# Joining the two words of a float64 weight with integer operations: six passes for ten

## The chip, the cores and the metric

The kernel runs on one core of a Trainium2 chip as one program. The time is the device time of that core in microseconds (us), the median over the runs. Five engines work at the same time, each through its own instructions in a fixed order: TensorE (PE, with its weight loads shown apart as PEld), VectorE (DVE), ScalarE (ACT), GpSimd (POOL) and SyncE (SP). SP does nothing here but issue DMAs. An instruction waits for what it needs on semaphores, and what stands behind it on the same engine waits too.

## The reference, cut to what matters

Three stages follow each other. The attention stage first lets 32 packed queries attend to 576 keys for each of 4 x 8 heads, and then lets the 576 queries attend to the 32 results. Its output, 2304 tokens of 512 values, goes through a first MoE layer and then through a second one with eight experts and an iterated routing:

```
p_packed = sm_attn(p, k, v); out = sm_attn(q, p_packed, p_packed)
h = x @ w_in                              # 512 -> 2048
x = (h * clip(h + 3, 0, 6) / 6) @ w_out   # 2048 -> 512
P = routing of x @ w_gate
out = sum over 8 experts of P[:, e] * (relu(x @ w1[e]) @ w2[e])
```

The two weight matrices of the first layer, `w_in` (512 x 2048) and `w_out` (2048 x 512), come as float64: 8 bytes for each element, 16.8 MB together. All else is float32.

## The kernel before, in words

**The planner.** The program is not written in the order in which it runs. Each operation is put into `Order` with an assumed cost on an engine (`t_act`, `t_dve`, `t_pool`, `t_pe`), with the buffers it reads, writes and fills, and with a priority (a smaller number goes first). `Order.run` then takes, again and again, the operation that can start first by those assumed costs, and among equals the one with the smaller priority. That gives every engine its order of instructions, SP's queue of loads included. An operation made with `alt` may go to POOL or to DVE; it goes to DVE if it would end there earlier by a margin. A buffer is a slot of a small set (`place`); a new use of a slot waits until the last user of the old one has ended. So a change in what an operation is assumed to cost, or in which buffers it holds, moves the order of other work on all engines.

**Start of the program.** Eight attention units (two for each of four batches) load their `k`, `q` and `v` (L510, L527, L535), transpose them on PE through PSUM tiles `tp` (L557, L647, L667), and work through two softmaxes on DVE and ACT. A small copy `pd` on POOL (L543) and a masked copy `pt` on DVE (L579) stand ahead of each unit's first scores (L599). Meanwhile the weights of the groups 0 to 3 of the first layer are loaded and converted ("early" pieces). The first layer has 8 groups of 256 of the 2048 inner values, and a unit of its work (`layer1a`, `layer2a`: L890 to L892 and L928 to L930 on PE) takes 384 tokens and two groups. PE multiplies with each operand split into a high and a low part, three products for one. The attention stage has a higher priority than the matmuls of the first layer, which fill what PE has left over. The groups 4 to 7 are converted while the first layer runs. After it comes the second layer (L996 to L998 and L1055 to L1057), with float32 weights.

**The conversion.** A raw piece `raw` of 128 partitions x 512 values of 8 bytes (512 KB) is one DMA on SP's queue (L392). There are two slots for `raw`, so the third load waits until the first piece has been used for the last time, and what stands behind it in SP's queue, the loads of `k`, `q` and `v` too, waits with it. There are 32 pieces: 16 early ones, each converted as one split of 512 values in `m_early` tiles, and 16 later ones, each as two splits of 256 values in `m` tiles. So there are 16 splits of 512 and 32 splits of 256. Each split holds two tiles (`m` and `t`) out of four.

The high word of a float64 holds the sign, 11 bits of exponent and the top 20 bits of the fraction; the low word holds 32 more bits. A split takes ten passes before. ACT makes the absolute value of the high word, read as if it were a float32 (L353), its sign (L357), and the low word as a number times 2 to the -52 (L361). DVE clamps the absolute value to the range of float32 exponents (L364), shifts it left by three and flips two bits (L367), ACT clears the sign bit (L371), and DVE masks the power of two out (L373). Three joins (L348, on POOL or DVE) multiply the low part by that power, add it, and multiply by the sign. For `w_in` the result lies in `w1f`; for `w_out` it is then split into a high part (L428, ACT) and a low part (L433, POOL or DVE). A `raw` slot comes free after the last join of its piece.

Of the kernel before, what the change touches and what calls it, by code (L numbers as in the profile page):

```python
# [9 lines left out]
F32 = mybir.dt.float32  # L10
F32R = mybir.dt.float32r
AF = mybir.ActivationFunctionType
ALU = mybir.AluOpType
# [3 lines left out]
U32 = mybir.dt.uint32  # L17


def float_of(bits):  # L20
    return struct.unpack("f", struct.pack("I", bits))[0]


def as_f32(ap):
    return ap.bitcast(F32)
# [32 lines left out]
JOIN = 0.5  # L58
# [75 lines left out]
def t_dve(n, fast=False):  # L134
    return 0.065 + n / (1920.0 if fast else 960.0)


def t_act(n, psum=False):
    return (0.05 if psum else 0.095) + n / 1200.0


def t_pool(n):
    return 0.15 + n / 465.0
# [7 lines left out]
def tile_kernel(  # L151
# [16 lines left out]
    nc = tc.nc  # L168
# [20 lines left out]
    def pool(name, stack=ctx, **kw):  # L189
        return stack.enter_context(tc.tile_pool(name=name, bufs=1, **kw))  # L190

    const, dp, accp, hp, wp = (pool(n) for n in ("const", "dp", "accp", "hp", "wp"))
    ph = pool("ph", space=PSUM)
    one, two = ctx.enter_context(ExitStack()), ctx.enter_context(ExitStack())
# [68 lines left out]
    maskb = const.tile([128, 2, NP], F32, name="maskb")  # L263
    maskz = const.tile([128, 2, 2, D], F32, name="maskz")
    three = const.tile([128, 1], F32, name="three")

    order = Order()

# [9 lines left out]
    def hold(tag, shape, dt=F32):  # L278
        return Hold(res[tag], maker(tag, shape, dt, ("",)))
# [8 lines left out]
    def dve(cost, fn, **kw):  # L288
        return order.op([("DVE", cost, fn)], **kw)

    def act(cost, fn, **kw):
        return order.op([("ACT", cost, fn)], **kw)

    def gps(cost, fn, **kw):
        return order.op([("POOL", cost, fn)], **kw)
# [14 lines left out]
    def alt(cost_dve, cost_pool, fn, spare=0.0, **kw):  # L310

        return order.op(
            [
                ("POOL", cost_pool, lambda: fn(nc.gpsimd)),
                ("DVE", cost_dve, lambda: fn(nc.vector), spare),
            ],
            **kw,
        )
# [7 lines left out]
    LEAST = float_of(897 << 20)  # L326
    MOST = float_of(0x47EFF000)
# [7 lines left out]
    def split_f64(r, c0, n, w, at, prio, halves, tag):  # L335

        words = lambda i: r.t.bitcast(U32).rearrange("p (n t) -> p n t", t=2)[:, c0:c0 + n, i]
        m = hold(tag, [128, n], U32)  # L340
        t = hold(tag, [128, n], U32)
        fast = t_dve(n, True)
        kw = dict(prio=prio)
        ts = nc.vector.tensor_scalar

        def join(dst, i0, i1, how, **deps):
            return alt(
                t_dve(n), t_pool(n), lambda e: e.tensor_tensor(dst(), i0(), i1(), how),  # L348
                spare=JOIN, **deps, **kw,
            )  # L350

        first = act(
            t_act(n), lambda: nc.scalar.activation(as_f32(m.t), as_f32(words(1)), AF.Abs),  # L353
            reads=[r], writes=[m], takes=[t], **kw,
        )
        sign = act(
            t_act(n), lambda: nc.scalar.activation(as_f32(words(1)), as_f32(words(1)), AF.Sign),  # L357
            takes=[r], after=[*r.writers[:1], first], **kw,
        )
        rest = act(  # L360
            t_act(n), lambda: nc.scalar.activation(as_f32(words(0)), words(0), AF.Copy, scale=2.0 ** -52),  # L361
            takes=[r], after=r.writers[:1], **kw,
        )
        dve(fast, lambda: ts(as_f32(m.t), as_f32(m.t), LEAST, MOST, ALU.max, ALU.min), writes=[m], **kw)  # L364
        dve(
            fast,
            lambda: ts(t.t, m.t, 3, 0xC0000000, ALU.logical_shift_left, ALU.bitwise_xor),  # L367
            reads=[m], writes=[t], **kw,
        )
        act(  # L370
            t_act(n), lambda: nc.scalar.activation(as_f32(t.t), as_f32(t.t), AF.Abs), writes=[t], **kw  # L371
        )
        dve(fast, lambda: ts(m.t, t.t, 0xFF800000, None, ALU.bitwise_and), reads=[t], writes=[m], **kw)  # L373
        mf, tf = (lambda: as_f32(m.t)), (lambda: as_f32(t.t))
        join(mf, lambda: as_f32(words(0)), mf, ALU.mult, takes=[r], writes=[m], after=[rest])
        join(tf, tf, mf, ALU.add, reads=[m], writes=[t])
        if halves:
            join(tf, tf, lambda: as_f32(words(1)), ALU.mult, takes=[r], writes=[t], after=[sign])
            split_part(at, tf, w, n, [t], prio)
        else:  # L380
            join(
                lambda: at(w.t), tf, lambda: as_f32(words(1)), ALU.mult,
                takes=[r], reads=[t], fills=[w], after=[sign],
            )

    def raw_piece(src, prio, tag="raw"):

# [9 lines left out]
    def whole(g, which, prio, tag, early=False):  # L397

        _, w1, w2, f0 = groups[g]
        if which == "w1":  # L400
            src = w1[:, f0:f0 + FG].rearrange("(c p) f -> p c f", p=128)
        else:
            src = w2[f0:f0 + FG, :].rearrange("(c p) d -> p c d", p=128)
        wide = src.dtype == I64
        shape = list(src.shape)
        w = hold(tag, shape) if which == "w1" else pair(tag, shape)
        per = shape[1] // (2 if wide else 1)
        for i in range(0, shape[1], per):
            r = raw_piece(src[:, i:i + per, :], prio, turn_of("raw", early))

            def at(t, i=i, c0=0, n=per * shape[2]):
                return t[:, i:i + per, :].rearrange("p c n -> p (c n)")[:, c0:c0 + n]

            if wide:
                n = DEC_EARLY if early else DEC
                for c0 in range(0, per * shape[2], n):
                    split_f64(
                        r, c0, n, w, lambda t, at=at, c0=c0, n=n: at(t, c0=c0, n=n), prio, which == "w2",
                        "m_early" if early else "m",
                    )  # L420
            else:
                split_part(at, lambda r=r: r.t, w, per * shape[2], [r], prio)
        return w

    def split_part(dst, src, w, n, deps, prio, **kw):

        high = act(
            t_act(n), lambda: nc.scalar.activation(dst(w.t[0]), src(), AF.Copy),  # L428
            reads=deps, fills=[w], prio=prio, **kw,
        )  # L430
        return alt(
            t_dve(n), t_pool(n),
            lambda e: e.tensor_tensor(dst(w.t[1]), src(), as_f32(dst(w.t[0])), ALU.subtract),  # L433
            reads=deps, fills=[w], after=[high], prio=prio, spare=SPARE,
        )
# [776 lines left out]
    with tc.manual_schedule():  # L1212
        nc.vector.memset(ones, 1.0)
        nc.vector.memset(three, 3.0)
        nc.vector.memset(maskb, 0.0)
        nc.vector.memset(maskb[0:64, 0, :], 1.0)
        nc.vector.memset(maskb[64:128, 1, :], 1.0)
# [20 lines left out]
        for gg in range(4):  # L1238
# [7 lines left out]
            writes=[wg], prio=90,  # L1246
# [81 lines left out]
```

## Time and profile before

| what | value |
|---|---|
| median of 3 runs | 1955.41 us (1952.35 to 1956.96) |
| span of the profiled execution | 1952.2 us |
| PE busy | 1915.1 us, 98% of the span |
| DVE, ACT, POOL busy | 62%, 50%, 49% |
| granted TensorE clock, mean | 0.998 |

The span reaches from the first to the last instruction of the profiled execution. The profile gives no separate device time for that execution; its span is 0.15 us under the fastest of the three runs and 3.2 us under their median. Busy shares are means over stages that differ: the conversion that is changed runs only in the first 310 us.

### The profile page before, as it was taken

How to read it: one execution, taken by the hardware profiler on the slowest of the kernel's cores; microseconds unless marked ns; L12 is line 12 of the kernel's file. 1: busy time of each engine (PE TensorE's matmuls, PEld its weight loads, DVE VectorE, ACT ScalarE, POOL GpSimd, SP SyncE). 2: the span in 40 equal slices, each digit the busy share in tenths (PEclk: the TensorE clock that was granted, in tenths of full speed). 3: DMA queues.
4: the chain of work that ended last, by engine and by line, in shares of the span. 5: the costliest groups of instructions: out<-in, count | busy, mean ns of one | idle time of the engine just before them, and what ended most of it. 6: DMA issues, size and time to landing. Idle time of an engine off the chain costs nothing.

```text
span 1952.2 us, 28194 instructions
## 1 busy us (share of the span) xinstructions
PE 1915.1 (98%) x10573; PEld 1735.2 (89%) x10573; DVE 1210.0 (62%) x1998; ACT 970.2 (50%) x2135; POOL 947.5 (49%) x987
## 2 busy tenths in 40 slices
PE   6999999999999999999999999999999999999998
PEld 4789999998899999999899999999999999999997
DVE  6996686447866676666755555555555555555554
ACT  6885674335455555555544443344444344443432
POOL 2444675236665666655634544435344343444431
PEclk9999999999999999999999999999999999999999
DMA  9931121001222222222310101111110111101102
GB/s 215 188 90 33 54 66 44 11 1 44 65 65 66 75 65 70 71 65 65 87 33 33 44 22 44 33 33 33 33 44 30 36 33 33 44 22 44 33 11 66
DMA packets 103546, 104.87 MB, mean 54 GB/s; under 512 B 42736, under 2 KB 78576, under 8 KB 103408
## 3 DMA queue, kind: packets, MB, share of 16 engines
q1 hardware_dynamic: 103408, 103.06, 19.4%
q8 instruction: 83, 1.36, 0.3%
q14 instruction: 55, 0.45, 0.1%
HBM read 98.32 MB, written 4.72 MB: 53 GB/s over the span
## 4 chain that ended last, share of the span: by engine, by line
PE 91%; DVE 5%; ACT 2%; DMA 1%; issue 1%; SPq 0%; POOL 0%; DVEq 0%; POOLq 0%; ACTq 0%
PE po L1055 13%; PE po L1056 13%; PE po L1057 13%; PE ph L996 12%; PE ph L998 12%; PE ph L997 12%; PE po L928 3%; PE po L930 3%; PE po L929 3%; PE ph L890 2%; PE ph L892 1%; PE ph L891 1%; PE ph L841 1%; DMA raw<-in_moe_w_out_dram 1%; DVE tmp L908 0%
## 5 line engine op out<-in xcount | busy, mean ns | idle before, releaser
L1079 DVE SCALAR_TENSOR_TENSOR acc<-po,Pr,acc 128x512 f32<-128x512 f32 x504 | 377.3, 750 | 287.2 <-PE po L1057 284.1
L433 POOL TENSOR_TENSOR hsl<-tmp,hsh 128x384 fp32r<-128x384 f32 x382 | 391.8, 1031 | 325.4 <-ACT hsh L428 272.4
L1055 PE MATMUL po<-w2h,hsh 128*128 128x512 f32 x1152 | 449.0, 390 | 0.0
L1056 PE MATMUL po<-w2l,hsh 128*128 128x512 f32 x1152 | 448.8, 390 | 0.0
L1057 PE MATMUL po<-w2h,hsl 128*128 128x512 f32 x1152 | 448.6, 389 | 0.0
L433 POOL TENSOR_TENSOR w1xl<-m,w1xh 128x256 fp32r<-128x256 f32 x152 | 111.5, 758 | 321.8 <-ACT w1xh L428 321.8
L1057 PEld LDWEIGHTS po<-w2h,hsl 128*128 128x128 f32 x1152 | 216.2, 188 | 45.3
L304 ACT ACTIVATE tmp<-ph 128x384 f32<-128x384 f32 x241 | 117.7, 489 | 274.8 <-PE ph L998 263.1
L1055 PEld LDWEIGHTS po<-w2h,hsh 128*128 128x128 f32 x1152 | 216.3, 188 | 41.8 <-DVE acc L1079 0.2
L1056 PEld LDWEIGHTS po<-w2l,hsh 128*128 128x128 f32 x1152 | 216.3, 188 | 41.5
L428 ACT ACTIVATE hsh<-tmp 128x384 fp32r<-128x384 f32 x480 | 242.4, 520 | 20.4 <-DVE tmp L908 12.6
L1010 DVE TENSOR_TENSOR tmp<-ph,tmp 128x384 f32<-128x384 f32 x288 | 159.8, 556 | 149.3 <-PE ph L998 129.7
L428 ACT ACTIVATE w2h<-raw 128x1024 fp32r<-128x1024 f32 x64 | 67.9, 1061 | 350.1 <-PE po L1057 338.1
L1018 ACT ACTIVATE tmp<-tmp 128x384 f32<-128x384 f32 x288 | 149.6, 520 | 87.2 <-DVE tmp L1010 82.8
L996 PE MATMUL ph<-ax,w1h 128*128 128x384 f32 x448 | 151.5, 338 | 3.3 <-DVE tmp L1010 3.3
L998 PE MATMUL ph<-ax,w1l 128*128 128x384 f32 x448 | 150.7, 336 | 0.0
L997 PE MATMUL ph<-ax,w1h 128*128 128x384 f32 x448 | 150.7, 336 | 0.0
L433 DVE TENSOR_TENSOR hsl<-tmp,hsh 128x384 fp32r<-128x384 f32 x98 | 105.6, 1078 | 42.0 <-ACT hsh L428 39.8
L433 POOL TENSOR_TENSOR w1l<-raw,w1h 128x512 fp32r<-128x512 f32 (+1 forms) x104 | 116.3, 1132 | 7.5 <-ACT w1h L428 6.8
L996 PE MATMUL ph<-xyh,w1h 128*128 128x384 f32 x320 | 108.3, 339 | 3.6 <-ACT tmp L304 3.6
L455 POOL TENSOR_TENSOR m<-raw 128x256 f32<-128x256 f32 x58 | 44.5, 770 | 138.7 <-DMA raw<-in_moe_w_dram 136.0
L998 PE MATMUL ph<-xyh,w1l 128*128 128x384 f32 x320 | 108.1, 338 | 0.0
(207 smaller groups left out, 4040.4 us busy)
## 6 DMA issues: line engine op xcount, KB each, us to landing
raw<-in_moe_w_dram SPq DMA_DIRECT2D x128, 512.0 KB, 3.5
raw<-in_moe_w_in_dram SPq DMA_DIRECT2D x16, 512.0 KB, 3.9
raw<-in_moe_w_out_dram SPq DMA_DIRECT2D x16, 512.0 KB, 3.6
k<-in_k_dram SPq DMA_DIRECT2D x32, 144.0 KB, 5.9
q<-in_q_dram SPq DMA_DIRECT2D x32, 144.0 KB, 4.5
v<-in_v_dram SPq DMA_DIRECT2D x8, 576.0 KB, 6.5
out_dram<-acc SPq DMA_DIRECT2D x36, 128.0 KB, 2.3
p<-in_p_dram SPq DMA_DIRECT2D x1, 224.0 KB, 5.7
```

What stands on the lines that cost most here:

```text
L304: ("ACT", t_act(n, True), lambda: nc.scalar.activation(dst(), src(), AF.Copy)),
L428: t_act(n), lambda: nc.scalar.activation(dst(w.t[0]), src(), AF.Copy),
L433: lambda e: e.tensor_tensor(dst(w.t[1]), src(), as_f32(dst(w.t[0])), ALU.subtract),
L996: nc.tensor.matmul(out, wh[:, at + c, :], bh[:, c, :], start=first and c == 0, **on)
L997: nc.tensor.matmul(out, wh[:, at + c, :], bl[:, c, :], start=False, **on)
L998: nc.tensor.matmul(out, wl[:, at + c, :], bh[:, c, :], start=False, **on)
L1010: t_dve(n), lambda: nc.vector.tensor_tensor(u.t, ps.t[:, :n], u.t, ALU.add),
L1018: t_act(n, bool(ps)), lambda: nc.scalar.activation(c.t, src(), AF.Relu),
L1055: nc.tensor.matmul(ps.t, hh[:, f, ts], wh[:, f, :], start=(f == 0), stop=False)
L1056: nc.tensor.matmul(ps.t, hh[:, f, ts], wl[:, f, :], start=False, stop=False)
L1057: nc.tensor.matmul(ps.t, hl[:, f, ts], wh[:, f, :], start=False, stop=(f == NFC - 1))
L1079: lambda row=row, share=share, ps=ps: nc.vector.scalar_tensor_tensor(row(), ps.t, share(), row(), ALU.mult, ALU.add),
```

## The change

The sum of a shifted high word and a rounded low word now makes the float directly, as an integer. ACT turns the low word into `2.0 + low * 2^-51` (a float whose bit pattern is 0x40000000 plus the low word's top bits, rounded), with the 2.0 as a bias out of a new tile `two`, and makes the absolute value of the high word as before. DVE clamps as before and shifts left by three, now without the flip. A new DVE operation with three operands takes the sign bit of the high word and sets it into the rounded low word. An integer add on POOL joins the two. This add has no choice of engine. `raw` is last read by the new DVE operation.

```diff
-        def join(dst, i0, i1, how, **deps):
-            return alt(
-                t_dve(n), t_pool(n), lambda e: e.tensor_tensor(dst(), i0(), i1(), how),
-                spare=JOIN, **deps, **kw,
-            )
-        first = act(
+        def join(dst, **deps):
+            return gps(
+                t_pool(n), lambda: nc.gpsimd.tensor_tensor(dst(), m.t, t.t, ALU.add), **deps, **kw,
+            )
+        low = act(
+            t_act(n) + 0.1,
+            lambda: nc.scalar.activation(as_f32(words(0)), words(0), AF.Identity, bias=two_, scale=2.0 ** -51),
+            takes=[r], after=r.writers[:1], **kw,
+        )
+        act(
             t_act(n), lambda: nc.scalar.activation(as_f32(m.t), as_f32(words(1)), AF.Abs),
             reads=[r], writes=[m], takes=[t], **kw,
         )
-        sign = act(
-            t_act(n), lambda: nc.scalar.activation(as_f32(words(1)), as_f32(words(1)), AF.Sign),
-            takes=[r], after=[*r.writers[:1], first], **kw,
-        )
-        rest = act(
-            t_act(n), lambda: nc.scalar.activation(as_f32(words(0)), words(0), AF.Copy, scale=2.0 ** -52),
-            takes=[r], after=r.writers[:1], **kw,
-        )
         dve(fast, lambda: ts(as_f32(m.t), as_f32(m.t), LEAST, MOST, ALU.max, ALU.min), writes=[m], **kw)
+        dve(fast, lambda: ts(m.t, m.t, 3, None, ALU.logical_shift_left), writes=[m], **kw)
         dve(
-            fast,
-            lambda: ts(t.t, m.t, 3, 0xC0000000, ALU.logical_shift_left, ALU.bitwise_xor),
-            reads=[m], writes=[t], **kw,
-        )
-        act(
-            t_act(n), lambda: nc.scalar.activation(as_f32(t.t), as_f32(t.t), AF.Abs), writes=[t], **kw
-        )
-        dve(fast, lambda: ts(m.t, t.t, 0xFF800000, None, ALU.bitwise_and), reads=[t], writes=[m], **kw)
-        mf, tf = (lambda: as_f32(m.t)), (lambda: as_f32(t.t))
-        join(mf, lambda: as_f32(words(0)), mf, ALU.mult, takes=[r], writes=[m], after=[rest])
-        join(tf, tf, mf, ALU.add, reads=[m], writes=[t])
+            t_dve(n),
+            lambda: nc.vector.scalar_tensor_tensor(
+                t.t, words(1), 0x80000000, words(0), ALU.bitwise_and, ALU.bitwise_or
+            ),
+            takes=[r], writes=[t], after=[low], **kw,
+        )
         if halves:
-            join(tf, tf, lambda: as_f32(words(1)), ALU.mult, takes=[r], writes=[t], after=[sign])
-            split_part(at, tf, w, n, [t], prio)
+            join(lambda: t.t, reads=[m], writes=[t])
+            split_part(at, lambda: as_f32(t.t), w, n, [t], prio)
         else:
-            join(
-                lambda: at(w.t), tf, lambda: as_f32(words(1)), ALU.mult,
-                takes=[r], reads=[t], fills=[w], after=[sign],
-            )
+            join(lambda: at(w.t).bitcast(U32), reads=[m, t], fills=[w])
...
+        nc.vector.memset(two_, 2.0)
```

## Rows read from the trace of the kernel before

**Rows 1.** Page: busy us, share of the span and instructions of each engine.

```profile
PE 1915.1 (98%) x10573; PEld 1735.2 (89%) x10573; DVE 1210.0 (62%) x1998; ACT 970.2 (50%) x2135; POOL 947.5 (49%) x987
```

**Rows 2.** Windows: PE, PEld, DVE, ACT, POOL busy, clock, DMA share, GB/s.

```profile
0.00:14.00 14.00, 2.86 (x13) 2.06 (x14) 8.25 (x22) 7.34 (x13) 2.42 (x8) 1.00 0.98 205
14.00:40.00 26.00, 20.74 (x220) 14.92 (x221) 18.26 (x52) 17.31 (x47) 7.62 (x10) 1.00 1.08 220
40.00:80.00 40.00, 35.19 (x375) 27.47 (x376) 36.37 (x98) 35.13 (x93) 20.71 (x19) 1.00 1.00 194
110.00:150.00 40.00, 38.11 (x287) 34.02 (x282) 36.57 (x78) 32.82 (x76) 19.49 (x20) 1.00 0.27 81
250.00:310.00 60.00, 58.54 (x360) 54.03 (x359) 55.02 (x106) 42.92 (x109) 45.24 (x53) 1.00 0.23 68
310.00:1952.20 1642.20, 1629.82 (x8390) 1481.55 (x8388) 963.90 (x1460) 748.76 (x1592) 783.47 (x804) 1.00 0.15 44
```

**Rows 3.** Waits of PE, first 150 us: total us, times, longest.

```profile
PE tp L557 <- DMA k<-in_k_dram: 9.9, 3, 7.8
PE tp L599 <- DVE pt L579: 2.1, 2, 1.8
PE tp L574 <- POOL pd L543: 1.4, 2, 0.9
```

**Rows 4.** Waits of SP's queue, first 150 us.

```profile
SPq L392 <- DVE m_early L348: 14.5, 4, 9.5
SPq L392 <- DVE w1f L348: 12.8, 4, 8.9
```

**Rows 5.** Timeline: start, us, engine, line, operation [idle before <-releaser].

```profile
12.96 0.69 DVE L348 TENSOR_TENSOR w1f<-m_early,raw 128x512 f32<-128x512 f32 x1
13.57 0.28 DVE L579 TENSOR_TENSOR pt<-tp,maskb 128x128 f32<-128x128 f32 x1
...
27.86 0.35 SPq L392 DMA_DIRECT2D raw<-in_moe_w_out_dram  x1
...
35.60 0.27 PE L557 MATMUL tp<-ident,k 96*128 96x96 f32 x1 [1.56 <-DMA k<-in_k_dram]
```

**Rows 6.** Windows of L348 alone: DVE and POOL busy in each.

```profile
0.00:140.00 140.00, 22.58 (x26) 27.61 (x21) 1.00 0.79 167
140.00:310.00 170.00, 26.84 (x32) 50.59 (x66) 1.00 0.19 56
```

**Rows 7.** Groups by line and form: times, busy us, mean ns; the other removed passes.

```profile
L357 ACT ACTIVATE raw<-raw 128x512 f32<-128x512 f32 x16 | 11.0, 689 | 0.0
L371 ACT ACTIVATE m_early<-m_early 128x512 f32<-128x512 f32 x16 | 10.2, 639 | 0.3 <-DVE m_early L367 0.2
L373 DVE TENSOR_SCALAR m_early<-m_early 128x512 uint32<-128x512 uint32 x16 | 8.8, 552 | 1.5 <-ACT m_early L371 1.1
L357 ACT ACTIVATE raw<-raw 128x256 f32<-128x256 f32 x32 | 14.1, 440 | 0.5
L371 ACT ACTIVATE m<-m 128x256 f32<-128x256 f32 x32 | 13.3, 416 | 14.0 <-DVE m L367 13.6
L373 DVE TENSOR_SCALAR m<-m 128x256 uint32<-128x256 uint32 x32 | 13.4, 417 | 5.7 <-ACT m L371 5.3
```

**Rows 8.** Instructions of the tiles: ns min/median/max, first and last start.

```profile
L348 DVE TENSOR_TENSOR m_early<-raw,m_early x10: 682/693/1674, 8.4 to 137.7; 128x512 f32<-128x512 f32 x10
L348 POOL TENSOR_TENSOR m_early<-raw,m_early x6: 1295/1306/1312, 30.3 to 123.3; 128x512 f32<-128x512 f32 x6
L348 DVE TENSOR_TENSOR m<-raw,m x9: 414/923/1287, 186.7 to 291.7; 128x256 f32<-128x256 f32 x9
```

**Rows 9.** Groups by form: an activation with a bias tile, and one without.

```profile
L903 ACT ACTIVATE tmp<-ph,three 128x384 f32<-128x384 f32 x96 | 55.5, 578 | 87.3 <-PE ph L892 86.2 <-DVE ax L433 0.8
L937 ACT ACTIVATE acc<-po 128x384 f32<-128x384 f32 x24 | 11.6, 484 | 6.1 <-PE po L930 6.0
```

**Rows 10.** DMA issues, first 140 us: KB each, median us to landing.

```profile
raw<-in_moe_w_out_dram SPq DMA_DIRECT2D x8, 512.0 KB, 4.8
```

More of the change, by code (lines that the diff above doesn't have):

```diff
@@ L265, in tile_kernel @@
     three = const.tile([128, 1], F32, name="three")
+    two_ = const.tile([128, 1], F32, name="two")
     order = Order()
@@ L355, in split_f64 @@
         )
-        sign = act(
-            t_act(n), lambda: nc.scalar.activation(as_f32(words(1)), as_f32(words(1)), AF.Sign),
-            takes=[r], after=[*r.writers[:1], first], **kw,
-        )
-        rest = act(
-            t_act(n), lambda: nc.scalar.activation(as_f32(words(0)), words(0), AF.Copy, scale=2.0 ** -52),
-            takes=[r], after=r.writers[:1], **kw,
-        )
-        dve(fast, lambda: ts(as_f32(m.t), as_f32(m.t), LEAST, MOST, ALU.max, ALU.min), writes=[m], **kw)
-        dve(
-            fast,
-            lambda: ts(t.t, m.t, 3, 0xC0000000, ALU.logical_shift_left, ALU.bitwise_xor),
-            reads=[m], writes=[t], **kw,
-        )
-        act(
-            t_act(n), lambda: nc.scalar.activation(as_f32(t.t), as_f32(t.t), AF.Abs), writes=[t], **kw
-        )
-        dve(fast, lambda: ts(m.t, t.t, 0xFF800000, None, ALU.bitwise_and), reads=[t], writes=[m], **kw)
-        mf, tf = (lambda: as_f32(m.t)), (lambda: as_f32(t.t))
-        join(mf, lambda: as_f32(words(0)), mf, ALU.mult, takes=[r], writes=[m], after=[rest])
-        join(tf, tf, mf, ALU.add, reads=[m], writes=[t])
+        dve(fast, lambda: ts(as_f32(m.t), as_f32(m.t), LEAST, MOST, ALU.max, ALU.min), writes=[m], **kw)
+        dve(fast, lambda: ts(m.t, m.t, 3, None, ALU.logical_shift_left), writes=[m], **kw)
+        dve(
+            t_dve(n),
[3 more added lines that the diff above has]
+            takes=[r], writes=[t], after=[low], **kw,
+        )
         if halves:
-            join(tf, tf, lambda: as_f32(words(1)), ALU.mult, takes=[r], writes=[t], after=[sign])
-            split_part(at, tf, w, n, [t], prio)
-        else:
-            join(
-                lambda: at(w.t), tf, lambda: as_f32(words(1)), ALU.mult,
-                takes=[r], reads=[t], fills=[w], after=[sign],
-            )
+            join(lambda: t.t, reads=[m], writes=[t])
+            split_part(at, lambda: as_f32(t.t), w, n, [t], prio)
+        else:
+            join(lambda: at(w.t).bitcast(U32), reads=[m, t], fills=[w])
     def raw_piece(src, prio, tag="raw"):
```

## The prediction

> **What bounds the kernel now.** I read the page first, then the windows by stage, then who waits for whom on PE and on SP's queue, and last the single passes of the conversion.
>
> PE is busy for 1915.1 of 1952.2 us [rows 1], so all its idle time is 37.1 us, and a change to the conversion can gain no more than the part of it that the conversion causes. The windows say where it lies [rows 2]: 11.1 us in the first 14 us, 5.3 from 14 to 40, 4.8 from 40 to 80, 1.9 from 110 to 150, 1.5 from 250 to 310, and 12.4 after 310, where nothing is converted any more. The granted clock is 1.00 in all these stretches but the last, so there is nothing to win from the clock.
>
> Of the first 14 us, 9.9 us in three waits (one of them later) are PE waiting for the first `k` loads [rows 3]; the change does not touch their start. The other 1.8 us there is one wait for `pt` on DVE [rows 3]. `pt` stands behind joins of the conversion in DVE's order: one ends as `pt` begins [rows 5], and two more of the same kind run in front of that one. So the idle time in reach is 1.8 + 5.3 + 4.8 + 1.9 + 1.5 = 15.3 us, 0.8% of the whole. That is the ceiling, however much work the change removes.
>
> Which engine makes PE wait in those stretches? From 40 to 80 us DVE is busy 36.4 of 40 us and ACT 35.1; from 110 to 150 DVE 36.6 of 40; from 250 to 310 DVE 55.0 of 60 [rows 2]. There DVE is close to full, and attention's small steps, which PE needs, stand in its order between conversions. From 14 to 40 DVE has 18.3 of 26 us and ACT 17.3: no engine is full; the DMA share is 1.08, and PE waits for loads and for chains of small steps. In that stretch the conversion acts through SP's queue: SP waits for the last join before it may load the next `raw`, 14.5 us and 12.8 us in eight waits for joins on DVE alone [rows 4], and loads of `k` and `q` stand behind. One case can be followed to PE: SP loads `raw` at 27.86 as soon as a join has ended, the next `k` goes after it, and PE waits 1.56 us for `k` at 35.60 [rows 5].
>
> **The change part by part.** Early splits (16 of 512 values, to about 140 us):
> - ACT loses the sign and the second absolute value, 11.0 + 10.2 = 21.2 us [rows 7]. The low word's pass stays, but gets a bias tile. An activation with a bias tile took 578 ns where one without took 484 on the same shape and source memory [rows 9], so I add 0.09 us for each, 1.5 us in all. Net 19.7 us off.
> - DVE loses the mask, 8.8 us [rows 7], and its 26 joins, 22.6 us [rows 6]. The clamp stays; shift-and-flip becomes shift alone, same pass and same price. It gains 16 three-operand operations, which the trace does not show with two SBUF inputs. The nearest row is the join that reads the same strided words, 682 to 1674 ns, median 693 [rows 8]. So 16 cost 11 to 27 us. The upper end belongs to instructions that ran beside POOL, and POOL will have less to do; I take 0.8 us, 13 us. Net 18 us off (4 to 20).
> - POOL loses 21 joins, 27.6 us [rows 6], and gains 16 integer adds. The trace shows no integer add on POOL. Its float joins took 1295 to 1312 ns [rows 8]; I take 1.3 us, 21 us, and as bounds half and twice that, 10 to 42 us. Net 7 us off (15 more to 17 off).
>
> Late splits (32 of 256, from 140 to 310 us): ACT 14.1 + 13.3 - 32 x 0.09 = 24.5 us off [rows 7, 9]; DVE 26.8 + 13.4 off and 32 x 0.41 to 1.29 on, with the median 0.92 a net of 11 off (27 off to 1 on) [rows 6 to 8]; POOL 50.6 off and 32 x about 0.75 on (50.6 over 66 joins is 0.77), 26 off [rows 6].
>
> The time of one early split, pass after pass, matters for the `raw` slots. Before: 0.69 + 0.43 + 0.43 + 0.64 + 0.43 for the first five in line, then three joins of 0.69 or 1.3: 4.7 to 6.5 us, and the slot is held to the end of it. After: 0.78 (low) + 0.69 (absolute value) + 0.43 + 0.43 + about 0.7 = 3.0 us to the last read of `raw`, and 1.3 more to the result. (0.69 and 0.64 are ACT's passes in [rows 7], the first taken for the first absolute value too; for the short DVE passes I take 0.43, under the mean of 0.55 in [rows 7], which holds instructions that were held up.) So the slot is free 1.7 to 3.5 us sooner even without a shorter queue.
>
> What comes out of it on PE, by stretch: the joins in front of `pt` shrink from three of 0.69 to one, 1.4 of the 1.8 us. From 14 to 40 I count only the wait for `k` that I could follow, 1.5 of 5.3 us; the rest is chains of attention and transfers at a DMA share above one. From 40 to 80 there are about five splits; each gives DVE 1.1 us and ACT 1.2 us, so their shares fall from 0.91 and 0.88 to about 0.77 and 0.73, and I take half of the idle time, 2.4 of 4.8 us (none if attention's own chain decides, all if the matmuls of the first layer, which fill gaps, get their weights sooner). Half also from 110 to 150 and from 250 to 310, 0.9 and 0.7 us. The new `memset` is one small DVE operation hidden under the first load. Sum: 1.4 + 1.5 + 2.4 + 0.9 + 0.7 = 6.9 us, bounds 0 and 15.3.
>
> The profiled span, 1952.2, would become 1945.3 us; the median of the runs is 3.2 us above that span, so from 1955.4 I come to **1948.5 us**.
>
> Where a join may go, POOL costs more than DVE: 1306 against 693 ns for the same join [rows 8], and the change leaves the last join no choice. The Trainium skill, GPSIMD Engine Reference, section Engine selection, speaks against that: ordinary elementwise work with two inputs belongs on VectorE, POOL being about twice as slow. By that rule the new add is the wrong step; the trace agrees on the factor (1.9).
>
> **The rivals.**
> 1. *Hidden anyway.* The waits belong to attention's chains and to its loads, and less work on DVE only makes it wait longer. For it: from 14 to 80 us the DMA share is 1.08 and 1.00 [rows 2]; PE's named waits there are for `k` and for attention's own steps [rows 3]. Against it: DVE at 0.91. It gives a gain of 0 to 3.5 us, 1952 to 1955.4.
> 2. *Weights loaded too soon (slower).* The planner sees `raw` come free sooner and puts its loads, which have the better priority, further ahead of `k` and `q` in SP's queue. Each such load takes 4.8 us to land in this stretch [rows 10], with the DMA engines full. If two of them hit a `k` that PE waits for, 9.6 us are lost against 6.9 gained: 1958 us. It decides from one and a half loads on. For it: PE already waits for a `k` that follows a `raw` [rows 5]. Against it: SP waits less for the joins [rows 4].
> 3. *The add holds POOL's queue (slower).* POOL works in order; behind an add that waits for DVE stand `pd`, for which PE already waited 1.4 us [rows 3], and the low parts of the first layer's operands. If each of eight units loses one add, 1.3 us, that is 10.4 us against 6.9: 1959 us. It decides from five units on. Against it: POOL is busy only 20.7 of 40 us from 40 to 80 [rows 2] and loses work. This is where the rule above would show.
> 4. *Nearly all idle time in reach comes back.* 11 to 15 us, 1940 to 1944: the layer's matmuls start early enough to fill every gap, as they do later.
>
> **How the numbers follow.** Chances: forecast (a gain of 3.9 to 10 us) 0.54, hidden 0.24, loads too soon 0.08, POOL's queue 0.05, nearly all 0.09. About 0.2%, 3.9 us, is what a measurement of this kernel can tell from no change. Faster: forecast and rival 4, 0.63. Same: rival 1 and the milder cases of 2 and 3, 0.26. Slower: 0.11. The range takes the forecast, rival 1 and half of rival 4, and a little above the time before, as the runs themselves differ by 2 us: 1942.5 to 1956.5.
>
> **What would show it.** Right: ACT about 44 us and DVE about 29 us less busy up to 310 us; PE idle between 14 and 80 us down from 10.1 to about 6; SP's waits for joins gone, and shorter ones for the new DVE operation in their place; the first `po` matmuls of the layer sooner; no difference after 310 us. Wrong: the new DVE operation near 1.6 us; the add near 2.6 us; `raw` loads ahead of `k` with PE waiting for `k`; the 12.4 us of idle time after 310 us changed by a new order of the planner, which I set at nothing as no operation there changes.

## The result, and the profile after

The changed kernel is slower: 1976.29 us (median of 4 runs, 1973.56 to 1977.21) against 1954.99 us (4 runs, 1952.35 to 1956.96), a ratio of 1.0109 (1.0095 to 1.0123). That is 21 us in the direction that I had given 0.11, and 20 us above the end of my range. The profiled execution has a span of 1971.8 us, 19.6 more than before; the mean granted clock is 0.995.

The page's row of the engines, for the kernel after, answers to [rows 1]:

```profile
PE 1927.8 (98%) x10573; PEld 1749.4 (89%) x10573; DVE 1160.4 (59%) x1936; ACT 941.6 (48%) x2039; POOL 919.9 (47%) x954
```

The work was removed: DVE is busy 50 us less, ACT 29, POOL 28. But PE is busy 12.7 us *more*, with the same 10573 matmuls. So two things went wrong: PE waits longer, and its instructions take longer. The windows of the kernel after, with the columns of [rows 2], say where:

```profile
0.00:14.00 14.00, 1.19 (x6) 0.93 (x6) 6.49 (x20) 5.93 (x9) 4.14 (x9) 1.00 0.80 206
14.00:40.00 26.00, 16.30 (x119) 11.19 (x119) 18.21 (x43) 15.34 (x34) 13.80 (x14) 0.89 1.16 220
40.00:80.00 40.00, 35.38 (x368) 28.75 (x367) 27.13 (x81) 29.30 (x79) 11.66 (x14) 0.95 0.93 193
80.00:110.00 30.00, 26.87 (x286) 22.95 (x285) 26.12 (x69) 23.64 (x62) 14.33 (x12) 1.00 1.03 209
110.00:150.00 40.00, 39.86 (x354) 36.04 (x353) 22.30 (x71) 23.43 (x63) 6.94 (x8) 1.00 0.20 50
310.00:1971.80 1661.80, 1649.63 (x8448) 1499.98 (x8446) 962.00 (x1466) 754.14 (x1598) 784.42 (x805) 1.00 0.14 43
```

The last row is the one to read first. After 310 us nothing is converted, and yet this stretch is 19.6 us longer than in [rows 2], with as little idle time (12.2 us, before 12.4). It has 58 more matmuls, 8448 against 8390: the first 310 us got that much less done. At 194 ns each (1629.82 us over 8390, [rows 2]) they are 11.3 us. And each takes longer, 1649.63 us over 8448, 195.3 ns, so 1.0 ns times 8448, 8.5 us. So the 21 us have two parts of about the same size: **a bad start** (11 us), and **slower matmuls to the very end** (8 to 9 us), in code that the change does not touch.

*The bad start.* From 0 to 14 us PE is idle 12.8 us (before 11.1), from 14 to 40 us 9.7 (before 5.3). From 40 to 80 us and from 110 to 150 it is idle a little less than before, 4.6 and 0.1 us (before 4.8 and 1.9). From 80 to 110 us it is idle 3.1 us; [rows 2] leave that stretch out, and there the kernel before shows

```profile
80.00:110.00 30.00, 29.90 (x308) 26.49 (x308) 27.16 (x69) 23.82 (x65) 10.12 (x9) 1.00 0.67 151
```

so 0.1 us. Up to 310 us that makes 31.8 us of idle time (310 less 1927.8 - 1649.63), 7.1 more than the 24.7 before. The other 4 of the 11 us are busy time in which less got done, in the stretches in which the clock is under 1.00. The waits of PE in the first 150 us (total, times, longest) name what it waits for; [rows 3] had 9.9 us for `k`, and no row for `q`:

```profile
PE tp L547 <- DMA k<-in_k_dram: 19.3, 6, 7.6
PE tp L637 <- DMA q<-in_q_dram: 2.5, 1, 2.5
```

Why `k` comes late is seen in SP's queue, in the timeline (start, us, engine, line, operation, count). First the kernel before:

```profile
0.74 0.95 SPq L392 DMA_DIRECT2D raw<-in_moe_w_in_dram  x2
1.73 3.45 SPq L510 DMA_DIRECT2D k<-in_k_dram  x4
...
8.92 0.62 SPq L535 DMA_DIRECT2D v<-in_v_dram  x1
11.22 2.88 SPq L392 DMA_DIRECT2D raw<-in_moe_w_in_dram  x2
14.19 2.90 SPq L510 DMA_DIRECT2D k<-in_k_dram  x4
```

Then the kernel after:

```profile
0.74 0.95 SPq L382 DMA_DIRECT2D raw<-in_moe_w_in_dram  x2
1.73 2.35 SPq L500 DMA_DIRECT2D k<-in_k_dram  x3
7.40 1.75 SPq L382 DMA_DIRECT2D raw<-in_moe_w_in_dram  x2
9.20 0.58 SPq L500 DMA_DIRECT2D k<-in_k_dram  x1
...
12.66 4.16 SPq L382 DMA_DIRECT2D raw<-in_moe_w_out_dram  x2
...
18.13 0.62 SPq L525 DMA_DIRECT2D v<-in_v_dram  x1
21.01 2.15 SPq L382 DMA_DIRECT2D raw<-in_moe_w_out_dram  x2
23.26 2.73 SPq L500 DMA_DIRECT2D k<-in_k_dram  x4
```

Count the loads of `raw` that stand ahead of the others: two ahead of the first unit's `v` before, six after; four ahead of the second unit's `k` before, eight after. The first unit's own fourth `k` stands behind four. A split of six passes gives its slot back sooner, in the planner's costs too, so the planner put the next `raw` load, which has the better priority, ahead of attention's loads. SP also stood still for a slot, from 4.08 to 7.40 us, with the fourth `k` behind it. Its waits in the first 150 us for the operation that now reads `raw` last (total, times, longest) take the place of [rows 4]. For the early pieces they are shorter, but there are more of them:

```profile
SPq L382 <- DVE m_early L365: 15.3, 11, 3.2
```

(One of 46.2 us for a late piece, tile `m`, ends at 190.68 us, when no load of attention is left behind it.)

PE's timeline (in brackets the idle time before the instruction, and what ended it) shows the price. The first unit's second group of transposes, before:

```profile
9.58 1.19 PE L557 MATMUL tp<-ident,k 96*128 96x96 f32 x6 [0.60 <-DMA k<-in_k_dram]
```

Both groups, after:

```profile
7.63 1.19 PE L547 MATMUL tp<-ident,k 96*128 96x96 f32 x6 [7.63 <-DMA k<-in_k_dram]
15.74 1.19 PE L547 MATMUL tp<-ident,k 96*128 96x96 f32 x6 [6.92 <-DMA k<-in_k_dram]
```

The second group, which needs the fourth `k`, starts at 15.74 us instead of 9.58.

The granted clock is no longer 1.00 throughout the first 310 us. Windows of 2 us of PE alone in the kernel after (busy, count, clock, DMA share, GB/s):

```profile
32.00:34.00 2.00, 0.63 (x5) 1.00 1.34 175
34.00:36.00 2.00, 0.79 (x5) 0.53 1.14 216
36.00:38.00 2.00, 1.27 (x5) 0.50 1.25 203
```

Behind 2 us in which PE has 0.63 us of work the clock falls from 1.00 (2.4 GHz) to 0.50 (1.2 GHz), and it is back at about 41 us. It falls once more from 65 to 68 us.

*The slower matmuls.* Here are instructions of the tile `w1h` (weights of the second layer) on PE from 1000 to 1400 us, a stretch in which PE is busy all the time at clock 1.00 in both kernels: ns min/median/max, first and last start. First before, then after:

```profile
L996 PE MATMUL ph<-xyh,w1h x131: 336/336/336, 1009.2 to 1399.8; 128*128 128x384 f32 x131
```

```profile
L986 PE MATMUL ph<-xyh,w1h x126: 336/339/341, 1006.2 to 1398.2; 128*128 128x384 f32 x126
```

Same shape, same clock, same operands, 3 ns more each (the 512-wide matmuls of that layer, 389 ns on the average, stay within 1 ns). In 400 us PE gets through 2009 matmuls of all kinds, against 2022. The one thing that the change does to this stretch is to move its buffers: the new tile `two` is one float wide, takes 32 bytes of every partition as the program is built, and most tiles that are allotted behind it lie 32 bytes further on (`w1h` at byte 112576 of a partition for 112544, and with it `w1l`, `raw`, `m`, `tmp`, `acc`, `w2`). So `w1h` begins 32 bytes past a multiple of 64 before, and on a multiple of 64 after.

### The profile page after: what moved, and what is told of

The parts are those of the page before. It is cut to its first block, busy times and chain, and to the rows that moved or that the text cites. A ratio compares the mean times of both kernels' runs of the same rounds, so it can differ in the third digit from the quotient of the medians.

```text
span 1971.8 us, 27983 instructions
## 1 busy us (share of the span) xinstructions
PE 1927.8 (98%) x10573; PEld 1749.4 (89%) x10573; DVE 1160.4 (59%) x1936; ACT 941.6 (48%) x2039; POOL 919.9 (47%) x954
## 4 chain that ended last, share of the span: by engine, by line
PE 92%; DVE 3%; DMA 2%; ACT 1%; issue 0%; POOL 0%; SPq 0%; DVEq 0%; ACTq 0%; POOLq 0%
PE po L1045 13%; PE po L1046 13%; PE po L1047 13%; PE ph L986 12%; PE ph L988 12%; PE ph L987 12%; PE po L918 3%; PE po L920 3%; PE po L919 3%; PE ph L880 2%; PE ph L882 2%; PE ph L881 2%; PE ph L831 1%; DMA k<-in_k_dram 1%; DMA raw<-in_moe_w_in_dram 1%
## 5 line engine op out<-in xcount | busy, mean ns | idle before, releaser
L423 DVE TENSOR_TENSOR hsl<-tmp,hsh 128x384 fp32r<-128x384 f32 x95 | 100.5, 1058 | 42.0 <-ACT hsh L418 36.0
L987 PE MATMUL ph<-xyl,w1h 128*128 128x384 f32 x320 | 109.0, 341 | 0.0
```

Source lines behind the costliest of these rows:

```text
L987: nc.tensor.matmul(out, wh[:, at + c, :], bl[:, c, :], start=False, **on)
```

## The experiments

Three causes were on the table. **Place**: the 32 bytes cost the second layer its pace. **Order of the loads**: the planner's new SP queue starves PE at the start. **The passes themselves**: six passes instead of ten are worth something, or cost something, if nothing else changes. A fourth came up with the first profiles: **the clock**, which falls when PE has waited. Each experiment has its ratio to the kernel before, run beside it on the same chip.

**1. The place alone.** The kernel before gets the new tile, and nothing uses it.

```diff
     three = const.tile([128, 1], F32, name="three")
+    two_ = const.tile([128, 1], F32, name="two")
...
+        nc.vector.memset(two_, 2.0)
```

> The kernel before, with nothing but the new 4-byte tile `two` and its memset, which nothing reads. The planner's order is the same, but the tiles that lie behind the small constants move up by 32 bytes. In the changed kernel the second layer's 128x384 matmuls took 339 to 341 ns in the mean where they took 336 to 338 before, at a granted clock of 1.00 in both, and between 310 us and the end the same kind of work took about 10 us more. Theory A (the place of the tiles in SBUF slows these matmuls): 1963 to 1967 us, 1.004 to 1.006 of before, with means of 339 to 341 ns. Rival (the slower pace comes from the order of work or from the slow start): 1955 us, 1.000, with 336 to 338 ns.

Measured: 1965.79 us, 1.0054 (1.0042 to 1.0067), 10.6 us lost by a tile that nobody reads. PE alone, from 310 to 1900 us (busy, count, clock, DMA share, GB/s), in the kernel before:

```profile
310.00:1900.00 1590.00, 1582.87 (x8159) 1.00 0.14 43
```

and in this one, with a row of `w1h` from 1000 to 1400 us:

```profile
310.00:1900.00 1590.00, 1582.90 (x8106) 1.00 0.15 43
```

```profile
L997 PE MATMUL ph<-xyh,w1h x124: 336/339/342, 1014.1 to 1390.4; 128*128 128x384 f32 x124
```

PE is equally busy and gets 53 matmuls less done; 53 x 194 ns are 10.3 of the 10.6 us. The 339 ns are those of the kernel after. So the place is a cause by itself, and the second part of the loss is found. It has nothing to do with the passes.

**2. The change without the move.** `three` and the new constant share one tile.

```diff
-    three = const.tile([128, 1], F32, name="three")
-    two_ = const.tile([128, 1], F32, name="two")
+    both = const.tile([128, 2], F32, name="three")
+    three, two_ = both[:, 0:1], both[:, 1:2]
```

> The changed kernel, with the constants three and two as the two columns of one 8-byte tile, so that no tile behind them moves. Theory A (place of the tiles): about 10 us back, 1965 to 1968 us, 1.005 to 1.007 of before, and the idle time of PE in the first 110 us stays (about 30 us). Rival (order of work): 1976 us as the changed kernel.

Measured: 1965.53 us, 1.0049 (1.0037 to 1.0062): 0.6% better than the changed kernel. PE still waits 17.5 us for `k` and 3.1 us for `q` in the first 150 us. The bad start is a second cause, independent of the first.

**3. The change with the old order of loads.** In the planner, the first 90 loads on SP's queue are held to the order of the kernel before; all else is left to it.

```diff
+SP_ORDER = [74, 75, 0, 1, 2, 3, 4, 5, 6, 7, 8, 9, 78, 79, 10, 11, 12,
...
             for o in self.open:
+                if o.ways[0][0] == "SP" and SP_ORDER[self.sent:] and SP_ORDER[self.sent] != o.nth:
+                    continue
...
             self.open.remove(o)
+            self.sent += o.ways[0][0] == "SP"
```

> The changed kernel, with the first 90 loads on SP's queue held to the order that they had before; the constants still move the tiles. Theory B (raw loads that the planner puts ahead of k and q cost the start about 12 us, idle PE time and a lower clock after it): PE's waits for k fall from 19 us to about 10 or less, the clock is 1.00 again from 14 to 80 us, and the total is 1957 to 1964 us, 1.001 to 1.005 of before, what is left being the place of the tiles less a gain from the fewer passes. Rival (the fewer passes themselves slow the start, through POOL's queue or the new DVE operation): 1970 us or more.

Measured: 1963.95 us, 1.0044 (1.0031 to 1.0056). The waits for `k` fall to 8.3 us and the one for `q` is gone. So the order of the loads is worth 1.0109 to 1.0044, 12.7 us, with the tiles moved. The clock still falls (0.87 from 14 to 40 us, 0.91 from 40 to 80), where I had expected 1.00.

**4. The kernel before with the new order of loads.** The same edit the other way round, in the kernel before, with the order of the first 90 loads of the kernel after.

> The kernel before with its ten passes, but with its first 90 loads on SP's queue in the order of the changed kernel. Theory B (order of the loads): slower than before by 10 us or more, 1965 to 1975 us, 1.005 to 1.010, with PE's waits for k near 19 us or above. Rival (the order of the loads does no harm): 1955 us.

Measured: 1978.62 us, 1.0119 (1.0103 to 1.0134), 23.6 us lost, more than the change itself loses by it. PE's two largest waits in the first 150 us and one of the windows (the columns of [rows 2]):

```profile
PE tp L566 <- DMA k<-in_k_dram: 17.1, 2, 9.4
PE tp L656 <- DMA q<-in_q_dram: 7.2, 2, 6.9
```

```profile
14.00:40.00 26.00, 10.94 (x60) 7.70 (x62) 12.97 (x28) 14.14 (x30) 5.66 (x6) 1.00 0.55 135
```

With ten passes a slot stays taken longer, so what stands behind a `raw` load waits longer, and the DMA engines are half idle meanwhile (0.55). The order does harm by itself, with no new pass in the kernel and the clock at 1.00 there; with the new passes the same order costs less.

**5. Both undone.** The edits of 2 and 3 in one: what is left of the change is its passes.

> The changed kernel with both side effects taken out: constants in one tile, so that nothing moves, and the first 90 loads on SP's queue in the order of before. If the two are separate and add up, 1976.3 - 10.8 (from the run without the shift) - 12.3 (from the run with the old order of loads) = 1953 us, 0.998 to 1.000 of before, with PE's clock still falling to half twice between 28 and 70 us. If they overlap: 1957 us or more. The prediction's 1948.5 would need the whole gain that it named.

Measured: 1955.67 us in 11 runs, 1.0004 (0.9995 to 1.0013). The two causes are all of the loss that can be measured, and the passes themselves show no gain: not the 6.9 us of my sum. PE's idle time up to 310 us is 23.1 us, against 24.7 (310 less the 1915.1 - 1629.8 us of [rows 1, 2]), so 1.6 us of idle time came back. Windows and PE's waits in the first 150 us:

```profile
14.00:40.00 26.00, 21.35 (x210) 16.65 (x208) 16.49 (x47) 14.48 (x39) 5.47 (x8) 0.87 1.08 217
40.00:80.00 40.00, 36.59 (x389) 29.25 (x387) 34.06 (x96) 31.81 (x84) 16.29 (x15) 1.00 1.00 201
80.00:110.00 30.00, 27.92 (x262) 24.38 (x259) 19.69 (x58) 19.69 (x53) 7.52 (x8) 0.94 0.60 130
0.00:310.00 310.00, 286.92 (x2176) 256.62 (x2177) 204.46 (x484) 189.79 (x450) 139.50 (x153) 0.98 0.46 109
```

```profile
PE tp L556 <- DMA k<-in_k_dram: 8.9, 1, 8.9
PE tp L573 <- POOL pd L542: 2.4, 2, 1.4
PE tp L707 <- DVE ppz L693: 2.2, 3, 1.0
PE tp L646 <- ACT qT L314: 1.8, 1, 1.8
...
PE tp L598 <- DVE pt L578: 1.2, 2, 0.7
```

After the first `k`, PE waits for attention's own steps (`pd`, `ppz`, `qT`, `pt`), one after another, and their waits did not go away with more time to spare on the engines: up to 310 us DVE is busy 204 us and ACT 190, against 246 and 221 before (the differences of [rows 1, 2]). By 310 us PE has done 2176 matmuls, in the same window of the kernel before 2185: with 1.6 us more of busy time it did 9 less. The clock, which falls in this run too (0.62, 0.50, 0.50 and 0.67 in the four stretches of 2 us from 28 to 36 us, and 0.94 from 80 to 110 us), is the likeliest reason. The single runs allow an estimate of its price. Of the 86 runs of the kernel before, 57 had a mean clock of 0.998 and took 1954.3 us on the average, and 7 had 0.996 and took 1956.7: about 1.2 us for each 0.001. The 86 have 0.998 on the average and the 11 runs of this kernel 0.995, which by that is about 3 us. So a small gain of the passes may be hidden under a lower clock; no run sets the clock alone.

**6. The mechanism behind the order.** The kernel of 2, but the `raw` slot is held until the add has ended, one pass longer than the data need.

```diff
-                t_pool(n), lambda: nc.gpsimd.tensor_tensor(dst(), m.t, t.t, ALU.add), **deps, **kw,
+                t_pool(n), lambda: nc.gpsimd.tensor_tensor(dst(), m.t, t.t, ALU.add), takes=[r], **deps, **kw,
```

> The changed kernel without the move of the tiles, with the raw slot held until the integer add instead of the new DVE operation, 1.25 us later in the planner's clock. If it is the earlier release of raw that puts the loads ahead of k: about half of the 10 to 12 us comes back, 1957 to 1962 us. If it is the shorter conversion as a whole: 1965 us, as without the move.

Measured: 1957.16 us, 1.0015 (1.0006 to 1.0024), so 6.7 of the 9.6 us that 2 lost come back, by freeing a buffer *later*. SP's timeline in this kernel, behind its first two loads of `raw`, is most of the way back to the old order, and the wait for `k` is 8.4 us:

```profile
1.73 3.16 SPq L500 DMA_DIRECT2D k<-in_k_dram  x4
...
7.32 1.76 SPq L382 DMA_DIRECT2D raw<-in_moe_w_in_dram  x2
...
11.08 1.54 SPq L525 DMA_DIRECT2D v<-in_v_dram  x1
12.72 1.36 SPq L500 DMA_DIRECT2D k<-in_k_dram  x1
```

The four `k` of the first unit are together again, and four loads of `raw` stand ahead of the second unit's first `k`, as before; but four and not two stand ahead of the first unit's `v`. So most of the bad order came from the earlier release of `raw`; the 2.9 us that are left are not explained.

**7. Attention's loads ahead of the weights.** The kernel of 2, with a priority for the conversion of groups 0 and 1 behind that of the first units.

```diff
-        return (9.4, 9.4, 13.4, 14.4, 100, 100, 100, 100)[gg]
+        return (10.4, 11.4, 13.4, 14.4, 100, 100, 100, 100)[gg]
```

> The changed kernel without the move of the tiles, and with the early priorities 10.4 and 11.4 in place of 9.4 and 9.4 for the first two groups, so that the first attention unit's k, q and v go ahead of all raw loads; the planner is otherwise free. Theory B (order of the loads decides the start): PE's first wait for k falls from about 7.7 us by the 3 us that two raw loads take, and the total is 1945 to 1955 us, 0.995 to 1.000. Rival (the weights come too late for the layer's first matmuls, and PE waits for them instead): 1960 us or more.

Measured: 1956.0 us, 1.0008 (1.0000 to 1.0017). That is between my two expectations. It undoes the bad order, but does not beat the kernel before, although its start is far better. Its windows:

```profile
0.00:14.00 14.00, 7.61 (x50) 5.22 (x52) 3.74 (x19) 5.25 (x13) 0.99 (x7) 1.00 0.78 197
14.00:40.00 26.00, 18.41 (x185) 13.37 (x183) 21.09 (x50) 16.35 (x41) 10.79 (x12) 0.80 0.98 215
40.00:80.00 40.00, 34.12 (x299) 29.01 (x296) 29.62 (x85) 30.52 (x74) 12.21 (x12) 0.87 0.92 206
```

PE is busy 7.61 us of the first 14 (2.86 in [rows 2]), 4.75 more, and loses 2.3 and 1.1 us of it again up to 80 us; and at clocks of 0.80 and 0.87 the busy time is worth less: 299 matmuls from 40 to 80 us against 375.

**8 to 10. Keeping PE busy.** To see what the clock costs, the first four units get 16 more transposes of the identity each, 64 in all, into PSUM ahead of the real ones (16 for the 18 of an expectation). They go into the kernel of 5, the kernel of 7 and the kernel before.

```diff
+    def keep(u, ps, n):
+        for _ in range(n * (u in (0, 1, 2, 3))):
+            nc.tensor.transpose(ps.t[:, 384:512], ident, ident)
...
+                    keep(u, ps, 2)
...
+            keep(u, ps, 2)
...
+                keep(u, ps, 3)
```

> The changed kernel with both side effects undone (constants in one tile, old order of the first 90 loads), and in the first four attention units PE gets 18 extra 128x128 transposes of the identity into a part of a PSUM tile that nothing reads (two ahead of each of four key transposes, three ahead of each of two softmax transposes, two ahead of each of two ppz steps; near 0.15 us each, where PE is mostly idle). Theory C (less work on the other engines leaves PE's idle time in longer stretches, the clock falls to half after them, and that eats the gain): the clock is 1.00 up to 80 us and the total 1949 to 1953 us, 0.997 to 0.999 of before, against 1955.7 without the extra work. Rival (the lower clock costs nothing, because PE is not what the start waits for): 1956 us or more, by what the extra work costs.

> The changed kernel without the move of the tiles, with the first unit's k, q and v ahead of the raw loads as in the run with the priorities 10.4 and 11.4, and with the same extra transposes. Theory C: the clock, 0.80 and 0.87 in the two stretches up to 80 us without the extra work, is near 1.00, and the total is 1946 to 1952 us, 0.996 to 0.999. Rival: 1956 us or more.

> The kernel before with the same extra transposes in the first four units. Its clock was 1.00 all along, so theory C expects no gain: 1955 to 1960 us, 1.000 to 1.003. If the extra work helped here too by more than 2 us, the gain of the two runs beside it would not be the clock's.

Measured: in the kernel of 5, 1954.97 us, 1.0002 (0.9993 to 1.0010); in that of 7, 1955.54 us, 1.0008 (1.0000 to 1.0017); in the kernel before, 1958.85 us, 1.0022 (1.0013 to 1.0032). In the kernel of 5 the fall is gone where it was, as this row shows, and yet no time is won:

```profile
14.00:40.00 26.00, 22.08 (x248) 16.33 (x245) 18.53 (x57) 16.90 (x44) 7.06 (x10) 1.00 1.14 223
```

In the kernel of 7 the clock is still 0.80 from 14 to 40 us, and the gain that I expected of the clock came in neither of the two. The extra work costs the kernel before 4.3 us and these two nothing, so the difference between old and new passes is 0.2% with the extra work in both, and none without. Over their runs the kernel of 5 and the kernel before, both with the extra work, have the same mean clock, 0.997, and the one is 3.9 us ahead of the other. That fits a gain of the passes that the lower clock took away in the kernel of 5. But how much of the extra work falls into idle time need not be the same in both, and the profiled execution of the kernel before with it is the fastest of nine (1954.42 us), so that its trace does not show the 4.3 us: this stays an argument.

**11. Which tiles the place matters for.** In the kernel before, a gap ahead of the tiles that are allotted late, in the room of attention's buffers: `w1h` and `w1l`, the first of the two slots of `w1xh` and `w1xl`, the later slots of `tmp` and `acc`, and the routing's tiles. All of these move by 32 bytes, and nothing else does.

```diff
         late, late_ps = pool("late"), pool("late_ps", space=PSUM)
+        late.tile([128, 1], F32, tag="gap0", name="gap0")
```

> The kernel before, with a 4-byte tile put first into the pool of the late tiles only, so that the second layer's w1 tiles, some of tmp and acc and the routing tiles move by 32 bytes, while raw, hs, w2 and all tiles of the first stages stay. If the stationary operand w1 of the 128x384 matmuls is what the place slows: 1963 to 1966 us, as when all tiles moved. If it is hs, w2 or raw: 1955 us.

Measured: 1963.47 us, 1.0044 (1.0032 to 1.0056). From 310 to 1900 us PE is busy as long as before and does 8113 matmuls, 46 less; up to 310 us it does as many as before. Most of the loss hangs on these late tiles.

**12 to 14. Is it the distance, or the place within 64 bytes?** Three kernels: the kernel before with an unused tile of 64 bytes at the place of `two` (all tiles move by 64); with a gap of 64 bytes ahead of the late tiles alone; and with `two` at its place (32) and a gap of 32 ahead of the late ones, so that the late tiles move by 64 and the others by 32.

```diff
+    two_ = const.tile([128, 16], F32, name="two")
```

```diff
+        late.tile([128, 16], F32, tag="gap0", name="gap0")
```

```diff
+        late.tile([128, 1], F32, tag="gap0", name="gap0")
...
+    two_ = const.tile([128, 1], F32, name="two")
```

> The kernel before, with an unused tile of 64 bytes in the place of the 4-byte one, so that the tiles behind it move by 64 bytes instead of 32. If what counts is how the tiles lie within 64 bytes: 1955 us, 1.000 of before, with 128x384 matmuls at 336 to 338 ns. If any move away from the old place costs: 1965 us, as with 32 bytes.

> The kernel before, with the late tiles alone (w1 and w1x of the second layer, some tmp and acc, the routing) moved by 64 bytes. If the place of these tiles within 64 bytes is the cause: 1955 us, 1.000 of before, against 1963.5 with 32 bytes, and 2020 or more matmuls from 1000 to 1400 us. If every move of these tiles costs: 1960 us or more.

> The kernel before, with the late tiles moved by 64 bytes and all others behind the constants (raw, m, hs, w2, tmp, acc) by 32. If the late tiles' place within 64 bytes is the whole cause: 1955 us. If hs, w2 or raw carry a part of the 10.6 us that all tiles together cost: 1956.5 to 1958 us, what the late tiles alone left over (1.7 us), or more.

Measured, in this order: 1959.58 us, 1.0028 (1.0017 to 1.0039); 1956.11 us, 1.0010 (1.0001 to 1.0019); 1957.82 us, 1.0019 (1.0010 to 1.0028). The row of `w1h` from 1000 to 1400 us in the second of them:

```profile
L997 PE MATMUL ph<-xyh,w1h x130: 334/334/336, 1009.9 to 1398.0; 128*128 128x384 f32 x130
```

So the late tiles cost 0.44% when moved by 32 bytes and 0.10% when moved by 64, and the matmuls of `w1h` are then as fast as before or faster: what counts is mostly where they lie within 64 bytes, not that they moved. The other tiles, moved by 32, cost at most 0.2%. The first of the three agreed with neither expectation: `w1h` was back at 335 ns, but 5.2 us were lost all the same. In its profile some 10 matmuls are missing by 310 us (2175 for 2185, as in the third) and 9 from there to 1900 us (8150 for 8159); the cause of that is open.

Which of the late tiles is it? The kernel of 11 holds the comparison in itself: of the two slots of `w1xh` one moved by 32 bytes and the other stayed, and the tiles that `w1xh` and `w1h` are multiplied with, `xyh`, `xyl` and `ax`, lie at the same place in all these kernels. The order of the matmuls in the built program tells which slot each one reads. From 1000 to 1400 us of its trace, a matmul with the slot that stayed starts 173.2 ns ahead of the next one on the average (156 of them), one with the slot that moved 176.6 ns (156 too); in the kernel before it is 173.2 ns for both slots. So the pace goes with the place of the weights that a matmul reads. No run moved one tile alone, and why the place matters no run shows.

## Why the prediction was wrong

The loss adds up from the runs: taking the place out of the changed kernel brings it from 1.0109 to 1.0049, taking the order of loads out as well brings it to 1.0004. In us: 11.7 and 8.8, and 0.8 for the passes, where zero is inside the interval. In the other order it is 12.7 for the loads and 7.8 for the place. The two prices differ by which is taken out first, by 3.9 us or 0.2%; the four ratios are known to 0.1% each, so that can be chance.

- **"The new `memset` is one small DVE operation hidden under the first load"** and **"no difference after 310 us"**: wrong, and the error that no rival covered. The operation is hidden; the tile that it fills is not. It moved other tiles by 32 bytes, which the sum put at nothing, and cost 10.6 us by itself, nearly all of it after 310 us. I read the diff for the instructions that it adds and not for the memory that it takes.
- **"The slot is free 1.7 to 3.5 us sooner"**: right, and I booked it as a gain. It was the cause of the other loss. **Rival 2** had the mechanism, the place and the sign (weights loaded ahead of `k` and `q`, PE waiting for `k`), and I gave it 0.08. Its condition, one and a half loads in front of a `k` that PE waits for, was passed by far: four more `raw` loads stand ahead of the first unit's `v` and the second's `k`. Its price of 9.6 us was near the measured 8.8 to 12.7. My argument against it, that SP would wait less for joins, was no argument: the longest such wait for an early piece did fall, from 9.5 to 3.2 us, but a queue in which more loads of the other kind stand in front starves PE all the same. The trace of before could have warned me: `raw` has the better priority (9.4, against 10 and up for attention), and what had kept its loads back was only the slow conversion.
- **From freed work to idle time of PE** (6.9 us in five terms): not borne out. With place and order taken out, the passes give no gain in time (1.0004, 0.9995 to 1.0013), and 1.6 us less idle time. This is near **rival 1**: the waits left are attention's chains. In that run's five stretches of the sum the idle time fell by 0.3, 0.6, 1.4, 1.1 and 0.6 us, where I had booked 1.4, 1.5, 2.4, 0.9 and 0.7: the two last terms were near, the three first too large (at the start the waits for `pt` fell only from 2.1 to 1.2 us; DVE's busy share from 40 to 80 us fell from 0.91 to 0.85, not to 0.77). Of these 4.0 us, 2.0 went again from 80 to 110 us, where PE waits 1.8 us for `qT`, and 0.4 from 150 to 250; the sum had no term for that, and why PE lacks work there no run shows.
- **"Nothing to win from the clock"**: true, but it can be lost. It was 1.00 in [rows 2] in every stretch up to 310 us and fell twice in the changed kernel, and also in the kernel of 5, at about 3 us by the estimate there.
- **The prices of the passes**: right. Here is what the new passes took in the kernel after (ns min/median/max, first and last start):

```profile
L365 DVE SCALAR_TENSOR_TENSOR m_early<-raw x16: 681/685/1140, 6.6 to 100.1; 128x512 uint32<-128x512 uint32 x16
L349 POOL TENSOR_TENSOR w1f<-m_early,m_early x8: 1258/1294/1641, 8.2 to 90.5; 128x512 uint32<-128x512 uint32 x8
```

I had taken 0.8 and 1.3 us, between bounds of 0.68 to 1.67 and 0.65 to 2.6. The low word's pass with its bias took 762 ns on the average, where I had 0.78 us. Up to 310 us DVE is busy 48 us less (I said 29; about half of the difference is my 0.92 us for the 256-wide form of the new operation, which took 0.66), ACT 34 (I said 44) and POOL 29 (33). ACT's passes did fall by 44.5 us in the groups: 48.6 off with the sign and the second absolute value [rows 7], 4.1 on with the low word's. But its instructions overlap by about 0.1 us where one follows the other, and with fewer in a row the busy time falls less than their sum.
- **Rival 3**, POOL's queue: PE's waits for `pd` were 1.4 us before and 2.4 us in the kernel of 5, 1.0 us more and not 10.4. The rule that stood beside it (the Trainium skill, GPSIMD Engine Reference, Engine selection: elementwise work with two inputs belongs on VectorE, POOL being about twice as slow) agrees with the trace on the price, 1294 ns for the integer add against 693 for the old join on DVE [rows 8]; the time did not hang on it. No run had the add on DVE.
- **Rival 4** did not come: no version beat the kernel before.

## What to carry to other kernels

A new constant is also a new address for most of what is allotted behind it: to judge an edit that allots anything, run the kernel before with that tile alone, or put the constant into a tile that is there. In a kernel whose queues are laid by a planner, a buffer that comes free sooner changes what is loaded first: compare the order of the loads ahead of adding up what the cheaper passes save. And time taken off an engine that is not the last to arrive is no gain; a term of such a sum should be booked only where one wait of the engine in question can be followed to the work removed.

## What the runs showed of the hardware

A matmul of 128x384 at clock 1.00 with PE busy throughout took 336 ns with its tiles in one place and 339 ns with them 32 bytes further, and 334 to 335 ns with them 64 bytes further; the 32 bytes cost half a per cent of the kernel (1.0054). In one and the same execution, matmuls that read a slot of weights that had moved by 32 bytes followed each other at 176.6 ns, and those with the slot that had stayed at 173.2. The granted clock fell from 1.00 to 0.50 behind stretches in which PE was mostly idle, and was back after some 3 to 7 us: in the kernel after from 34 to 41 us, behind 2 us with 0.63 us of work, and from 65 to 68 us, behind 2 us with 0.28. In the kernel before it stayed at 1.00 up to 310 us, although PE had 0.16 us of work from 12 to 14 us and 0.44 from 34 to 36. What tells these cases apart no run here shows.
